# One fixed-order region over the whole kernel, and six order strings laid out anew

## Chip, core and metric

The kernel runs on one core of a Trainium2 chip. The core has five engines that run side by side, each with its own instruction stream and waits on semaphores: TensorE (PE, matmuls; PEld is its weight load), VectorE (DVE), ScalarE (ACT), GpSimd (POOL) and SyncE (SP, which issues most of the DMAs). The metric is the device time of one launch in microseconds. The kernel before takes 396.76 us, the median of 3 runs (395.31 to 397.34).

## The reference

Four residual layers over x of shape 1 x 2048 x 512: attention, convolution, and both again with the same weights.

```python
def _A_ref(x, wqkv, wo):            # 32 heads of 16
    qkv = (x @ wqkv) ...
    off = jnp.arange(8) * 2         # 8 keys per row: itself and every second row behind it
    logits = jnp.einsum("bhsd,bhswd->bhsw", q, kg) * scale
    attn = _softmax(jnp.where(mask, logits, -1e9), axis=-1)
    o = jnp.einsum("bhsw,bhswd->bhsd", attn, vg)
    return o.reshape(B, S, D) @ wo

def _B_ref(u, A_re, A_im, B_re, B_im, C_re, C_im, log_dt, Dskip):
    P = jnp.exp(logdA[:, :, None] * l[None, None, :])
    K = jnp.einsum("dn,dnl,dn->dl", Cc, P, dB).real      # the kernel of a state space model
    Yf = rfft2(pad(u)) * rfft2(pad(K))
    return irfft2(Yf)[..., :L] + u * Dskip

x = x + _A_ref(_layernorm(x), A_wqkv, A_wo)
x = x + _B_ref(_layernorm(x), ...)
x = x + _A_ref(_layernorm(x), A_wqkv, A_wo)
x = x + _B_ref(_layernorm(x), ...)
```

## The kernel before

The program runs through six parts, one after the other, with the seams overlapped. The order of each part is a string in which a letter, or a letter with digits, stands for one step.

- k_gen (0 to about 104 us, string ORDERK) makes the convolution kernel K from tables of powers, and at the same time normalises x, transposes it and projects keys and queries. Its last steps are the first products of query and shifted key for the attention that follows.
- LayerA.core (about 104 to 180 us, string CORE0) is the first attention. For each of four query blocks q and four feature tiles ft, `mult` (letter m) multiplies the queries with 8 shifted copies of the keys on DVE (line 342, tile prod, two buffers); `lsum` (l) sums the products over a head's 16 features on PE with 8 matmuls (line 350) or 32 (line 354) into the logits L; `mx` (x) takes the maximum (line 414); then follow the exponential, the sum, the reciprocal and the normalised weights attn. `q_proj` (q) and `v_proj` (v) each do one projection of four matmuls (lines 223 and 398), which ACT casts out (lines 225 and 400). When the last rows of v are there, two DMAs copy v_ext shifted by one partition (lines 403 and 404). `pv_mult` (P) multiplies weights and shifted values on DVE (line 472, tile pav), `pv_sum` (S) sums on PE (lines 487 and 497), `out_proj` (O) projects (line 508).
- FftB.run with ORDER0 (about 180 to 237 us) is the first convolution, through transforms as matmuls: f1 (line 811; its outputs a1s are cast at line 800), f2 (line 818), `u_f2` (U, cast ub at line 869), the product with the spectrum of K `u_mult` (u, line 857, on DVE), and back with i1 (m, lines 883 and 887) and i2 (y and v, lines 931 to 933, then the sum into x_sb at lines 935 and 937). The spectrum of K (kf) is made here once and stored to kf_dram.
- ORDERF (about 237 to 262 us) ends the first convolution together with the layer norm, transposes (T; lines 271 and 273) and key projections (P; lines 282, 285 and 295) of the second attention. A digit behind a letter is a block or a tile.
- LayerA.core with CORE1 (about 262 to 343 us) is the second attention; `load_w2` issues 32 loads of w_sb on SP (line 596).
- FftB.run with ORDER1 (about 343 us to the end) is the second convolution. It loads the stored spectrum: `kf_load` issues three DMAs for each of 16 pieces (lines 847 and 849), up to 10 pieces ahead of the products, into the tiles named kf_ring, w_sb and kx. `store` writes finished rows to the output.

What sets the order of the work: `tc.manual_schedule(engines=...)` keeps the engines that it names in the order in which the program issues to them. Outside such a region, and across its edges, the scheduler may move instructions. MAN names DVE, ACT, PE and SP; MAN_ALL adds POOL. Before, there is one region with MAN_ALL around k_gen, and four with MAN: around the first core, around ORDER0, around ORDERF and CORE1 together, and around ORDER1. The loads of one DMA queue are issued in the queue's order: an issue that waits holds up those behind it.

## Time and profile before

The profiled execution has a span of 393.9 us; the median of the runs is 396.76 us, so some 2.9 us lie around the span.

| what | value |
|---|---|
| median of 3 runs | 396.76 us |
| span of the profiled execution | 393.9 us |
| DVE's instructions | 449 |
| share of DVE in the span | 95% |
| DMA moved | 54.18 MB, 138 GB/s on average |

The chain of work that ended last, which is followed back from the last instruction to what released each step, stands on these engines:

```profile
PE 49%; DVE 21%; ACT 19%; issue 5%; DMA 2%; SPq 2%; POOL 1%; DVEq 0%; ACTq 0%; POOLq 0%
```

The costliest lines on DVE are these; after the bar come the busy time and the mean of one in nanoseconds, then the idle time ahead of them and what ended it:

```profile
L472 DVE TENSOR_TENSOR pav<-attn,v_ext 128x4096 bf16<-128x4096 bf16 (+1 forms) x34 | 72.3, 2160 | 0.3 <-DMA v_ext<-v_ext 0.3
L342 DVE TENSOR_TENSOR prod<-qT,kT_ext 128x4096 bf16<-128x4096 bf16 x29 | 65.6, 2288 | 3.0 <-PE L L350 2.1
L1119 DVE TENSOR_TENSOR A_t<-A_t,pow_t 128x1024 bf16<-128x1024 bf16 (+4 forms) x46 | 38.2, 873 | 0.2
```

### The profile page before, as it was taken

The page shows a single profiled execution, that of the slowest core. Times are in us where ns is not written, and L with a number is a line of the kernel's source. Part 1 is how long each engine was busy: PE and PEld are TensorE (multiplying, and loading weights), DVE is VectorE, ACT ScalarE, POOL GpSimd, SP SyncE. Part 2 cuts the span into 40 slices and gives each one's busy share as a digit, 9 for nine tenths or more (in the row PEclk, how much of TensorE's full clock was granted, in tenths as well). Part 3 has the DMA queues.
Part 4 walks back from the last instruction along what each step waited for, and adds up shares of the span by engine and source line. Part 5 has one row for each costly group of instructions (what it writes and reads, how often), then busy time and mean ns, then how long its engine had stood idle before and what let it go on. Part 6 is the DMA issues. An engine that isn't in the chain of part 4 may idle for free.

```text
span 393.9 us, 14769 instructions
## 1 busy us (share of the span) xinstructions
PE 324.1 (82%) x6451; PEld 231.5 (59%) x6499; DVE 372.8 (95%) x449; ACT 331.1 (84%) x568; POOL 65.5 (17%) x97
## 2 busy tenths in 40 slices
PE   3000258999999999999998899999999999998894
PEld 2000116756734676766887888543456676677894
DVE  6999999999989999999999989979999999989984
ACT  7999999997558799899999998574666779889992
POOL 9402960000280000010731201100000020000000
PEclk9999999999999999999999999999999999999999
DMA  7953810414027556277678634820253057604525
GB/s 209 396 155 50 83 53 3 106 28 108 9 66 198 128 168 176 61 228 235 215 265 300 216 110 110 300 62 2 73 141 96 3 170 222 195 13 155 171 68 152
DMA packets 68303, 54.18 MB, mean 138 GB/s; under 512 B 33545, under 2 KB 58670, under 8 KB 67982
## 3 DMA queue, kind: packets, MB, share of 16 engines
q1 hardware_dynamic: 66566, 48.70, 42.7%
q0 software_dynamic: 1664, 4.52, 3.1%
q8 instruction: 51, 0.84, 0.9%
q14 instruction: 14, 0.11, 0.1%
q10 hardware_dynamic: 8, 0.00, 0.0%
HBM read 30.15 MB, written 13.24 MB: 110 GB/s over the span
## 4 chain that ended last, share of the span: by engine, by line
PE 49%; DVE 21%; ACT 19%; issue 5%; DMA 2%; SPq 2%; POOL 1%; DVEq 0%; ACTq 0%; POOLq 0%
PE pq L398 7%; PE po L497 5%; PE pq L508 4%; PE pq L223 4%; PE pk L1277 3%; DVE A_t L1119 3%; ACT ub L869 3%; DVE B_t L1119 3%; PE L L354 3%; PE pp L282 3%; ACT a1s L800 3%; PE pp L1215 2%; DVE t L857 2%; SPq L596 2%; PE L L350 2%
## 5 line engine op out<-in xcount | busy, mean ns | idle before, releaser
L472 DVE TENSOR_TENSOR pav<-attn,v_ext 128x4096 bf16<-128x4096 bf16 (+1 forms) x34 | 72.3, 2160 | 0.3 <-DMA v_ext<-v_ext 0.3
L342 DVE TENSOR_TENSOR prod<-qT,kT_ext 128x4096 bf16<-128x4096 bf16 x29 | 65.6, 2288 | 3.0 <-PE L L350 2.1
L1119 DVE TENSOR_TENSOR A_t<-A_t,pow_t 128x1024 bf16<-128x1024 bf16 (+4 forms) x46 | 38.2, 873 | 0.2
L1205 PE MATMUL pt<-ident,x_blk 128*128 128x128 bf16 x64 | 6.0, 241 | 39.4 <-ACT x_blk L195 39.4
L508 PE MATMUL pq<-wop,oT 128*128 128x512 bf16 x121 | 31.5, 379 | 2.4 <-issue 1.9
L497 PEld LDWEIGHTS <-pav 64*128 64x128 bf16 x1728 | 26.9, 95 | 9.9 <-DVE pav L472 3.3
L869 ACT CAST ub<-pb 128x1024 bf16<-128x1024 f32 x32 | 32.6, 1110 | 0.0
L1215 PE MATMUL pp<-xnT,kT_ext 128*128 128x512 bf16 x88 | 25.5, 413 | 7.3 <-ACT xnT L1208 4.3
L818 PE MATMUL pb<-a1s,w_sb 128*128 128x64 bf16 x768 | 27.4, 193 | 3.8 <-ACT ub L869 1.4
L398 PE MATMUL pq<-wv,xnT 128*128 128x512 bf16 x123 | 30.0, 379 | 0.5 <-ACT kgs L1285 0.3
L497 PE MATMUL po<-ident,pav 64*128 64x64 bf16 x1728 | 29.9, 190 | 0.6 <-ACT oT L499 0.2
L400 ACT CAST v_ext<-pq 128x512 bf16<-128x512 f32 x32 | 18.7, 586 | 13.5 <-PE pq L398 11.1
L800 ACT CAST a1s<-pb 128x1024 bf16<-128x1024 f32 x29 | 28.5, 1063 | 1.2 <-PE pb L811 1.2
L1205 PEld LDWEIGHTS <-x_blk 128*128 128x128 bf16 x64 | 4.6, 107 | 41.3 <-ACT x_blk L195 40.2
L818 PEld LDWEIGHTS <-w_sb 128*128 128x128 bf16 x768 | 25.1, 98 | 6.0 <-issue 4.0
L178 POOL TENSOR_TENSOR ln_rstd<-ln_rstd,ln_mh 128x4 f32<-128x4 f32 x2 | 4.0, 1995 | 120.1 <-DVE ln_rstd L177 66.9
L1277 PEld LDWEIGHTS <-A_t 128*64 128x64 bf16 (+1 forms) x512 | 21.7, 103 | 3.8 <-DVE A_t L1119 0.2
L800 DVE CAST a1s<-pb 128x1024 bf16<-128x1024 f32 x19 | 22.5, 1220 | 1.4 <-PE pb L811 1.0
L1277 PE MATMUL pk<-B_t,A_t 128*64 128x84 bf16 (+1 forms) x512 | 23.5, 201 | 0.2
L223 PE MATMUL pq<-xnT,kT_ext 128*128 128x512 bf16 x85 | 22.6, 379 | 0.9 <-issue 0.5
L225 ACT CAST qT<-pq 128x512 bf16<-128x512 f32 x24 | 14.0, 585 | 9.8 <-PE pq L223 9.5
L398 PEld LDWEIGHTS <-xnT 128*128 128x128 bf16 x128 | 11.9, 97 | 15.3 <-issue 2.4
(264 smaller groups left out, 919.9 us busy)
## 6 DMA issues: line engine op xcount, KB each, us to landing
w_sb<-w_dram SPq DMA_DIRECT2D x64, 128.0 KB, 3.0
w_dram<-xnT SPq DMA_DIRECT2D x1, 4096.0 KB
kf_ring<-kf_dram SPq DMA_DIRECT2D x13, 256.0 KB, 3.8
kf_ring<-kf_dram SPq DMA_DIRECT2D x26, 128.0 KB, 3.6
v_ext<-v_ext SPq DMA_DIRECT2D x4, 784.0 KB, 6.1
x_blk<-in_A_x_dram SPq DMA_DIRECT2D x4, 512.0 KB, 4.7
kT_ext<-in_A_wqkv_dram SPq DMA_DIRECT2D x4, 512.0 KB, 9.2
x_sb<-in_A_x_dram SPq DMA_DIRECT2D x4, 512.0 KB, 6.3
```

Of the source, the lines that this page charges most:

```text
L223: nc.tensor.matmul(pq[:], lhsT=self.wqk[:, dt, ft * P:(ft + 1) * P], rhs=self.xnT[:, dt, q * 512:(q + 1) * 512], start=(dt == 0), stop=(dt ...
L342: nc.vector.tensor_tensor(pr, self.qT[q][:, ft].unsqueeze(1).to_broadcast([P, W, 4, P]), kap, ALU.mult)
L398: nc.tensor.matmul(pp[:], lhsT=xnT[:, dt, a * P:(a + 1) * P], rhs=wv[:, dt, :], start=(dt == 0), stop=(dt == NDT - 1))
L472: nc.vector.tensor_tensor(pv[:, i], attn[:, n % 4].unsqueeze(2).to_broadcast([P, W, DH // parts, H]), vap, ALU.mult)
L497: nc.tensor.matmul(po[:, h, 0, i * nt + ft, :], lhsT=pvf[rows, i, w, ft * P:(ft + 1) * P], rhs=ident[rows, rows], start=(w == 0 and ft + i ...
L508: nc.tensor.matmul(pw[:], lhsT=oT[:, ftp, :], rhs=self.wo[:, ftp, :], start=False, stop=(ftp == NDT - 1))
L800: (self.nc.scalar.copy if eng == "act" else self.nc.vector.tensor_copy)(dst, src)
L818: nc.tensor.matmul(p2[:, j, :], lhsT=self.w2[:, ec * EC + j, :], rhs=a1s[:, ec * EC + j, :], start=True, stop=True)
L869: nc.scalar.copy(ub[:], p2)
L1119: return lambda: nc.vector.tensor_tensor(*args)
L1215: nc.tensor.matmul(pps[kind, b, ft][:], lhsT=la.wqk[:, dt, c:c + P], rhs=la.xnT[:, dt, b * 512:(b + 1) * 512], start=(dt == 0), stop=(dt = ...
L1277: nc.tensor.matmul(o, lhsT=lhs, rhs=Bt[:, ri, c * CH + ql].rearrange("p b g -> p (b g)"), start=(not half and j % 4 == 0 and ri == 0), sto ...
```

## The change

It has two halves. One `manual_schedule` with MAN is opened at the start of the function and stays open to its end; around k_gen a second one adds POOL alone, and the later regions become `if True:`. And all of the six order strings have their steps in another order; each string holds the same steps as often as before, so each engine runs the same instructions. LATE0, ROWS and ENGK stay. Lines behind the strings are one lower in the kernel after.

```diff
 ORDER0 = """
-KD KA KA KA KA KD KD KA KA KD kA KD KA KD KA kA kD UA KD UA UD UA UA UD UA UD
-kA KD kA kD u kD u m u kA kD UA UA m u kD UA kD m UA UA u m kD UA m
...
+KD KA KA KA KA KD KD KA KA KD KD kA kA kD KA KD KA KD UA UA UD UA KD UA UD UA UD kA kA kD u kD kA u
+m kD u m m UA u u kD u kD UA m m UA UA u m UA kD UA u UD UA m m kA kA u kD kA yD u u YA m YA m u m
...
 ORDER1 = """
-UD UA UA UD UA UD UA UD UA UD UA u UD m u m u u m UA u UA m u UD m
-UA m u m u u m u m u u m YA YD u YA m m yA YD m u u YA u YA
-YA m m m w001A w000D yA yA w011D YA w010D yA yD yA yD yA v102D v101A v112D v111A v113D v103D v100A v110D
+UD UA UA UD UA UD UA UD UA UD UA u UD u m u UA UA m UD m u u u m u m m UA m u m u u m u u m YA YD u
+YA m m yA YD u u m w001A u YA YA m YA m m w000D yA YA YA w010D yA yD yA yD yA v102D w011D v100A
+v110D v112D v113D v103D v101A v111A
 """
 CORE0 = """
-vmvvvvqlvmxvlmemvvrclvnlmqTlqmxmvvelvvvvcmlqcPlSPrqOmncml1VTxPPqeSmr2lqP4OlSOSm5PqOP3S7lmOSnlPOx
-VPeOPSPrOSnPO6SObbP9SwOP8SPdBHOVaOPfSEdObatSaCaAfataGDFO
+mmvvvvlvmvqlxmlevvmqvrllcnqqTmvvxlvvmvvvPqePclmSmlmrcO6lxncVqPTPeSOOPqSrl3SmP5qml4OS2OPlmS7nlPOx
+PVeOSbrOPSnPOSbP18OSPPOdSBOV9aEPdOPSfObGaCaFatfASOtaHaDw
 """
 CORE1 = """
-0m1l2ml3mqvvmvllqvmqvxqelmlvmmvvqrlnqlmTvmxPPvlvvqvvqvmlmvqlqelmSrqnxmPSPqTOSOSlePOlPmrSOSnmOOPl
-bSlPSPwOxdfPVaePOSraPOnVabPOSPdOSOPSbPOSfaOftSdafaaftO
+0mv21lm3lqvvmvmqllmvqqvmvxllvqevqmmrlmlvnvvmxTvqPlvlPvmveqqrmlSmnlSqxTPqOPmlSeqOSOOmPlrSPnbPlSOP
+SmOOSlPOxwVeOdrPSfPbnPVOadPaSOSPafOPSbOPaSfdaOSfataftO
 """
...
     nc = tc.nc
+    ctx.enter_context(tc.manual_schedule(engines=MAN))
...
-    with tc.manual_schedule(engines=MAN_ALL):
+    with tc.manual_schedule(engines={ET.Pool}):
         C = k_gen(tc, nc, ...
...
-    with tc.tile_pool(name="ctmp_g2", bufs=1) as g2tmp, tc.manual_schedule(engines=MAN):
+    with tc.tile_pool(name="ctmp_g2", bufs=1) as g2tmp:
...
-    with tc.manual_schedule(engines=MAN):
+    if True:
         late["."] = lambda: None
         fb.run(ORDER0, u, k=kp, late=[late[c] for c in LATE0.split()])
```

ORDERK (four lines of 96 letters) and ORDERF (the end of the first convolution) are permuted in the same way, and the regions around ORDERF with CORE1, and around ORDER1, become `if True:` too.

More of the change, by code (lines that the diff above doesn't have):

```diff
@@ L46 @@
 ORDERK = """
-sbiCCiCisCGiCbiMsaibsCbMiibMcMsTibMGicGMMbasMGiGibTMTMbsGGTabbiTTiaTsicGTbbacTiTibcGsTMTGiaGaMlM
-TbasMlWaiaMlyMMwyyiMiayMsttbeMkTaaaMadeMaiMkkaMKMTalMbMkMlWMMqMKqlqMqMMMyyQMHQyqqUQkkpyakKaUkKqt
-pUtUxUexqpQUaekdkUqUUaxaqUKUpUUk3axHUl3EkplTKpTWQ3Tl3xlTxTyppWyqyqkHxTlytkTTQqUzzeKqUTteQUkTkTKE
-kUTzkzUkTxkTKttkKkUkUkpKekekxKUUpkkKqxpKUqUUxUkUoEUUkpQkUKkpxUUoxpUXpxXKopxxZXZZ
+siCbCiCsibiCisibbMCsiMaiCMMbsTcaiMibbMTGTisMibbGsTcGbiMibaGMTiTsMcbcaTibaTTbiTasMMGaacaMiMGbaGla
+MaGGMMlGMGTwWMaTsiaTlyyMTayTylitMtaelqeWMMkMksMliqMQbykMMykKiMdKqyMqyaMQktMMtdMqkbMMHqeapKpxUUUU
+aUxapQapUqqkUkU3HaU3eUUQTxKUkkTqaUlqKxTkUkpQTTaxl3TEppW3TlqxpyKTyqykHTlytkTUUTWUtQTKeUUlqqkTUQkT
+UekKkkUUKxkKkzkkkzxzzppKtxeUUtpUkeKUkkkxxpKUkUKooUExpqUqkUpKUokkxEUpKXxQXpxxZXZZ
 """
 ORDER0 = """
-KD KA KA KA KA KD KD KA KA KD kA KD KA KD KA kA kD UA KD UA UD UA UA UD UA UD
-kA KD kA kD u kD u m u kA kD UA UA m u kD UA kD m UA UA u m kD UA m
-u u UD UA m u kA u m m kA kD kA m yD u m u YA m u YA yD u u m
-m YA u m u m w000A m YA yA YD YA yA yD yA w010D yA
+KD KA KA KA KA KD KD KA KA KD KD kA kA kD KA KD KA KD UA UA UD UA KD UA UD UA UD kA kA kD u kD kA u
+m kD u m m UA u u kD u kD UA m m UA UA u m UA kD UA u UD UA m m kA kA u kD kA yD u u YA m YA m u m
+yD u u m u m w000A m m u YA YA yA m YD YA yA yD yA w010D yA
 """
@@ L59 @@
 ORDERF = """
-yD h00 h01 yA YA v101A v100A v110A v111A h10 z12A a0 p0 v113A h11 a1 p1 z02A S z03A n0D T0 n1G E00D
-v103D E01A P03 H2 a2 T1 P01 E10D p2 E11D Q00 n2G H3 P00 a3 P02 P11 P12 p3 T2 E21D E20D P10 P13
-P22 P20 n3D T3 E31A P23 P21 E30D x1
+yD yA YA h01 v101A h00 v100A v110A h10 a0 v111A v113A p0 z02A S h11 z03A a1 p1 z12A n0D T0 n1G E00D
+v103D H2 E01A P00 T1 Q00 P03 a2 E10D p2 P02 E11D P13 n2G H3 a3 P01 P11 T2 E20D p3 P12 E21D P10 P20
+n3D P23 T3 E31A E30D P22 x1 P21
 """
 ORDER1 = """
-UD UA UA UD UA UD UA UD UA UD UA u UD m u m u u m UA u UA m u UD m
-UA m u m u u m u m u u m YA YD u YA m m yA YD m u u YA u YA
-YA m m m w001A w000D yA yA w011D YA w010D yA yD yA yD yA v102D v101A v112D v111A v113D v103D v100A v110D
+UD UA UA UD UA UD UA UD UA UD UA u UD u m u UA UA m UD m u u u m u m m UA m u m u u m u u m YA YD u
+YA m m yA YD u u m w001A u YA YA m YA m m w000D yA yA YA w010D yA yD yA yD yA v102D w011D v100A
+v110D v112D v113D v103D v101A v111A
 """
 CORE0 = """
-vmvvvvqlvmxvlmemvvrclvnlmqTlqmxmvvelvvvvcmlqcPlSPrqOmncml1VTxPPqeSmr2lqP4OlSOSm5PqOP3S7lmOSnlPOx
-VPeOPSPrOSnPO6SObbP9SwOP8SPdBHOVaOPfSEdObatSaCaAfataGDFO
+mmvvvvlvmvqlxmlevvmqvrllcnqqTmvvxlvvmvvvPqePclmSmlmrcO6lxncVqPTPeSOOPqSrl3SmP5qml4OS2OPlmS7nlPOx
+PVeOSbrOPSnPOSbP18OSPPOdSBOV9aEPdOPSfObGaCaFatfASOtaHaDw
 """
 CORE1 = """
-0m1l2ml3mqvvmvllqvmqvxqelmlvmmvvqrlnqlmTvmxPPvlvvqvvqvmlmvqlqelmSrqnxmPSPqTOSOSlePOlPmrSOSnmOOPl
-bSlPSPwOxdfPVaePOSraPOnVabPOSPdOSOPSbPOSfaOftSdafaaftO
+0mv21lm3lqvvmvmqllmvqqvmvxllvqevqmmrlmlvnvvmxTvqPlvlPvmveqqrmlSmnlSqxTPqOPmlSeqOSOOmPlrSPnbPlSOP
+SmOOSlPOxwVeOdrPSfPbnPVOadPaSOSPafOPSbOPaSfdaOSfataftO
 """
@@ L1494 @@
     la.front_w()
-    with tc.manual_schedule(engines=MAN):
+    if True:
         la.front_open()
@@ L1548 @@
     fb.open_mid()
-    with tc.manual_schedule(engines=MAN):
+    if True:
         out_v = out.rearrange("b (p a) d -> p (b a) d", p=P)
```

## The prediction

> **What bounds the kernel now.** I read the page's busy times first, then the busy time of each engine in stretches that match the kernel's parts, then VectorE's waits, and last the timelines around the places where the order changes.

> ```profile
> PE 324.1 (82%) x6451; PEld 231.5 (59%) x6499; DVE 372.8 (95%) x449; ACT 331.1 (84%) x568; POOL 65.5 (17%) x97
> PEclk9999999999999999999999999999999999999999
> ```

> VectorE (DVE) works 372.8 of 393.9 us. The change keeps every instruction, so DVE's 372.8 us stay and the most that any order could save is its 21.1 us of idle time. The stretches say where that idle lies; the columns are the length, then PE, PEld, DVE, ACT and POOL busy, the granted clock, DMA share and GB/s:

> ```profile
> 0.00:104.00 104.00, 53.35 (x651) 36.29 (x660) 99.74 (x167) 94.25 (x175) 31.89 (x46) 1.00 0.44 113
> 104.00:112.00 8.00, 7.68 (x85) 3.81 (x84) 6.42 (x5) 4.14 (x8) 5.95 (x11) 1.00 0.21 55
> 112.00:180.00 68.00, 65.65 (x1359) 42.37 (x1375) 67.67 (x44) 58.87 (x117) 6.17 (x11) 1.00 0.54 152
> 180.00:240.00 60.00, 55.26 (x1596) 50.00 (x1597) 58.12 (x75) 59.49 (x73) 15.03 (x25) 1.00 0.64 219
> 240.00:262.00 22.00, 21.37 (x175) 13.64 (x176) 19.21 (x59) 15.04 (x30) 3.50 (x4) 1.00 0.59 187
> 262.00:300.00 38.00, 37.48 (x376) 18.53 (x382) 36.76 (x21) 22.51 (x37) 0.00 (x0) 1.00 0.27 73
> 300.00:343.00 43.00, 41.73 (x1171) 29.79 (x1175) 42.39 (x35) 35.15 (x83) 2.94 (x1) 1.00 0.44 134
> 343.00:378.00 35.00, 31.19 (x749) 27.07 (x744) 33.60 (x43) 33.71 (x43) 0.00 (x0) 1.00 0.34 106
> 378.00:394.00 16.00, 10.37 (x334) 9.96 (x324) 8.91 (x10) 7.96 (x10) 0.00 (x0) 0.98 0.46 134
> ```

> The reader is to see that the bound moves. Up to 104 and in the two attention cores (112 to 180, 300 to 343) DVE is full; in 180 to 240 ACT is (59.49 of 60); in 240 to 300 PE is (21.37 of 22, 37.48 of 38); the last 16 us are a chain. Of DVE's idle 4.3 us lie before 104, 7.1 after 378, and 9.8 between, in pieces. DVE's largest waits in the middle name their causes:

> ```profile
> DVE x_sb L935 <- PE pb L933: 2.5, 6, 0.8
> DVE prod L342 <- PE L L350: 2.1, 2, 1.6
> DVE kT_ext L295 <- ACT kT_ext L285: 1.3, 2, 1.2
> DVE xnT L273 <- PE pt L271: 1.2, 2, 1.1
> ```

> **The change part by part.** *The region.* DVE's, ACT's and POOL's orders come from the strings in both kernels; compiled with the old strings, the single region moves only two things.

> First, the handoff from k_gen to the first core:

> ```profile
> 108.25 0.61 PE L350 MATMUL L<-A_pr,ind 128*32 128x512 bf16 x8
> 108.79 0.39 PE L398 MATMUL pq<-wv,xnT 128*128 128x512 bf16 x1
> 109.11 0.62 PE L350 MATMUL L<-A_pr,ind 128*32 128x512 bf16 x8
> 109.78 2.29 DVE L342 TENSOR_TENSOR prod<-qT,kT_ext 128x4096 bf16<-128x4096 bf16 x1 [1.57 <-PE L L350]
> ```

> Eight v_proj matmuls (L398) that the scheduler had put between the three groups of logit sums (L350) now come after the third. The groups then wait only for their products; the last of these ends at 108.0, a group lasts 0.6, so the product at 109.78 can start at about 108.83: DVE gains 0.95 us. PE pays: it stands from about 107.0 to 108.1, 1.1 us, where it did projections before. DVE is full behind this place, so a gain there carries on until some PE result is late: the next gates are the first pav (its shifted v_ext lands when DVE has about 0.3 left) and the last maximum of the logits at 138.8, which waits for PE. Bounds 0 and -0.95; I take -0.5, the middle, because half of the gates on the way hang on the engine that is later.

> [...]

> Second, SyncE's (SP's) queue in layer 1. Before, the load of g_sb and 7 of the first 10 kf_ring triples went out at 245.75 to 289, the two v_ext shifts between them. Now these 22 issues stand behind the shifts and the 32 w_sb loads. Rows:

> ```profile
> 281.46 0.67 SPq L403 DMA_DIRECT2D v_ext<-v_ext  x1
> 316.60 18.38 SPq L596 DMA_DIRECT2D w_sb<-w_dram  x32
> 337.19 0.52 SPq L847 DMA_DIRECT2D w_sb<-kf_dram  x1
> 337.75 1.30 SPq L849 DMA_DIRECT2D w_sb<-kf_dram  x2
> 357.06 0.45 SPq L847 DMA_DIRECT2D kf_ring<-kf_dram  x1
> ```

> A triple takes about 1.9 us to issue (337.2 to 343.5 for three is 2.1, 246.13 to 255.2 for four 2.3 at most, 357.06 to 358.9 is 1.85); from 335.4 on the ten are issued by 335.4 + 10 x 2.0 = 355.4, and kf_ring's next loads, which wait for the product at 357, are not passed over. Landing takes 2.5 to 5.9 us from issue. Load n is there at 337.4 + 2.0n + 5.9 at worst, and needed at 355.8 + 1.15n (L857's products): for n = 9, 361.3 against 367.2 (two casts in between). So 0, covered by 6 us; without that cover it is a rival below. The bounds are 0 and +3.8.

> *ORDERK.* DVE is full to 104; what moves is within its queue. The one gate that tightens is the table copy by ACT at 61.8: its slack of 0.6 us becomes -0.8 if ACT's work is merely counted up, but ACT had that much idle before it. Zero, bounds -0.3 and +0.5.

> *CORE0, ORDER0, ORDERF.* In the two latter the waits of 1.05 at 258 (PE, L271) and 1.16 at 260.8 (ACT, L285) have the same producers with the same work ahead of them; moves elsewhere stay within one or two instructions and cross no gate with less than 0.3 us. Zero, bounds -0.5 and +0.5.

> *CORE1.* Here PE is the bound and has no gaps, so a place in its order is a time. Projections of four matmuls (0.87 us each by PE's rows) were moved ahead of groups of L350. DVE's products wait for these, since their buffers come free only then:

> ```profile
> 271.76 2.29 DVE L342 TENSOR_TENSOR prod<-qT,kT_ext 128x4096 bf16<-128x4096 bf16 x1 [0.27 <-ACT v_ext L400]
> 282.78 4.49 DVE L342 TENSOR_TENSOR prod<-qT,kT_ext 128x4096 bf16<-128x4096 bf16 x2 [0.49 <-PE L L350]
> 303.23 4.49 DVE L472 TENSOR_TENSOR pav<-attn,v_ext 128x4096 bf16<-128x4096 bf16 x2 [0.26 <-DMA v_ext<-v_ext]
> ```

> Counting the work ahead of each, the L350 group that releases the product at 267.0 moves 0.9 later (it had 0.3 to spare: DVE +0.6), the one for 271.76 by 1.7 (0.1 to spare), for 277.79 by 1.3 (0.1), for 282.78 by 1.7 (0.1). These overlap, they don't add: DVE is 0.5, 1.2, 0.9 and 1.4 late there, and about 1.0 at the maximum at 299.55. At 303 a pav goes ahead of a product and the wait of 0.26 goes. From 303 to 343 DVE has 0.6 us of idle, so it can't catch up. I take +1.1; bounds 0 (if PE's queue has slack that the records miss) and +1.6, the largest single delay.

> *ORDER1.* To 378 DVE's order is the same but for one cast. In the tail a group of 16 matmuls (L931 to L933, 0.9 us) and its DVE sum go from ahead of the last inverse transforms (L887) to behind them. The chain of waits there is PE alone, so what DVE waited for at 379.7 (0.81) and 381.5 (0.56) comes 0.9 earlier; but the moved 0.9 us of PE are still owed before the last sum at 388.41. What can be won is what PE stands idle before that sum: its records after 378 add up to 10.37 us, all of 378 to 388.4, but counted at the pace of gapless matmuls (0.06 us for those of 128 columns) the work after 378.9 is 9.2 us, which ends at 388.1. I take -0.4, the 0.3 and a little for the shorter last sums; bounds -0.8 and +0.3.

> The sum: -0.5 + 0 + 0 + 0 + 1.1 - 0.4 = +0.2. The profiled span of 393.9 becomes 394.1; the median before is 396.76, 2.9 above the span, so 397.0 us.

> **The rivals.** A difference under 0.5%, 2 us, can hardly be told from none here, so the forecast is "same".

> *The gains carry, CORE1 is not later.* For it: the new order has several operands landing just as DVE comes for them (the pav ahead of the product at 303 starts as the second v_ext shift lands), as if PE had time to give there. Against it: four gates with 0.1 to 0.3 us of slack. -0.95 at the handoff, -0.5 in ORDER0 and ORDERF, -0.8 in the tail, 0 in CORE1, -0.3 in ORDERK: -2.55, so 394.2 us.

> *The late loads.* The single region puts the kf_ring loads behind w_sb. If a triple costs over 2.6 us with w_sb's own traffic still moving, load 9 comes later than its product (337.4 + 9 x 2.6 + 5.9 = 366.7 against 367.2): that is the point from which it decides. At 3.07 us (512 KB at the 170 GB/s of the slice with w_sb) it is 370.9, DVE 3.8 us late, and ACT and PE behind it: 400.5 us. Against it: the triples at 337 to 343 took 1.9 to 2.1 right behind the same w_sb loads.

> [...]

> *CORE1's delays add.* Each product waits for a sum and each sum for a product; if PE also stands at the late products, the 1.6 is paid twice, +3.2, with -0.9 at the handoff and in the tail not won since DVE comes late to both ends: 400.0 us. For it: PE has only 0.5 us of idle in 262 to 300. Against it: there are two product buffers, so a product is two groups ahead.

> *The region does nothing.* Then the handoff's gain and the queue's risk go; 397.5 us, and not told from the forecast.

> **How the numbers follow.** Forecast with the region rival 0.40, gains carry 0.30, late loads 0.13, delays add 0.17. Faster needs 394.8 or less: 0.30. Slower needs 398.7 or more: 0.30. The forecast's own range is 395.4 to 398.6. All terms at their lower bounds give 394.2, and the runs of before reach 1.45 us below their median; all but the queue's at their upper bounds give 396.8 + 0 + 0.5 + 0.5 + 1.6 + 0.3 = 399.7, and the late loads 400.5. I give 393.2 to 400.8.

> **What would show it.** Handoff: the L342 product that waited 1.57 us waits about 0.6. CORE1: waits of L342 on L350 between 265 and 285 that sum to over 1.5 us, and the last L472 some 1 us nearer the end of the span than the start would let it be. Queue: no wait of L857 on kf_ring. Tail: the waits of L935 on L933 fall from 2.5 to under 1.8. I am wrong if L857 waits for a DMA, if ACT's stretch 180 to 240 grows by over 0.5 us, or if CORE1's waits vanish.

## The result, and the profile after

The changed kernel is slower: 406.94 us, the median of 4 runs (404.60 to 408.59), against 396.03 us for the kernel before, run beside it (4 runs). The ratio is 1.0275, with a 95% interval from 1.0241 to 1.0308, so about +10.9 us. The forecast was 397.0 us, no change, with a range to 400.8. The profiled execution of the kernel after has a span of 405.6 us.

The line of busy times and the clock line of the page after, to be held against those of before:

```profile
PE 327.2 (81%) x6456; PEld 235.0 (58%) x6499; DVE 373.2 (92%) x449; ACT 331.0 (82%) x568; POOL 58.9 (15%) x97
PEclk9999998999999999999999999999998999999898
```

DVE's work is the same, 373.2 against 372.8 us; what was added is idle time, 32 us in place of 21. And the clock line, which was all 9s, has four places with 8 in it: the granted clock is halved from 61.09 to 64.50 us, from 306.85 to 310.26, from 375.12 to 378.53, and from 402.42 to the end. Six of the nine stretches of before, shifted with the work (the columns are the length, then PE, PEld, DVE, ACT and POOL busy, the granted clock, DMA share and GB/s):

```profile
0.00:107.00 107.00, 53.20 (x627) 35.70 (x634) 99.21 (x167) 93.22 (x173) 25.23 (x46) 0.98 0.43 110
107.00:115.00 8.00, 7.59 (x103) 4.54 (x102) 7.59 (x5) 4.29 (x8) 4.76 (x9) 1.00 0.14 37
266.00:306.00 40.00, 38.44 (x422) 19.85 (x427) 37.49 (x22) 23.49 (x39) 0.00 (x0) 1.00 0.18 47
306.00:351.00 45.00, 41.85 (x1073) 29.39 (x1085) 41.96 (x35) 34.01 (x81) 1.03 (x1) 0.96 0.38 116
351.00:388.00 37.00, 31.89 (x761) 28.11 (x755) 33.60 (x43) 33.38 (x42) 0.00 (x0) 0.95 0.76 235
388.00:406.00 18.00, 11.26 (x358) 10.71 (x355) 9.30 (x11) 8.69 (x11) 0.00 (x0) 0.90 0.40 119
```

The same work takes 3 us more up to the handoff, 1 us more in the first core (not shown) and 2 us more in each of the last four stretches; only the handoff (107 to 115) is better, with 0.4 us of DVE's idle time in place of 1.6. Two things to see in the last three lines: the granted clock of 0.96, 0.95 and 0.90, and the DMA share of 0.76 in the second convolution, where it was 0.34. The 0.90 costs nothing: PE's last matmul is over at 399.3, ahead of the last halved period.

Both kernels run the same DVE work, so the time at which DVE has done a given amount of it tells how late the new kernel is at each place of the program. Worked out from the two traces, in us after minus before:

```
place in the kernel before     DVE late by
k_gen, at 20 us                -0.1
k_gen, in the middle           +1.9
k_gen, end                     +2.8
handoff done                   +1.6
core 0, at 130                 +2.5
core 0, end                    +2.7
ORDER0, end                    +3.5
ORDERF, end                    +3.9
CORE1, at 296                  +5.3
CORE1, at 325                  +7.8
CORE1, end                     +7.9
ORDER1                         +9.6
tail                           +10.8
```

DVE's waits name the first losses (the columns are us in all, how often, and the longest):

```profile
DVE prod L341 <- PE L L349: 2.9, 4, 1.0
DVE a1s L799 <- PE pb L810: 2.3, 3, 1.0
DVE A_t L1118 <- DMA pow_t<-pow_t: 2.1, 1, 2.1
...
DVE B_t L1118 <- ACT B_t L1106: 1.1, 1, 1.1
```

The wait of 2.1 us for pow_t is new, and it is a wait for a DMA's landing in k_gen. The same product in the kernel before, and in the kernel after:

```profile
25.66 0.28 DVE L1119 TENSOR_TENSOR A_t<-A_t,pow_t 128x256 bf16<-128x256 bf16 x1
```

```profile
24.92 0.49 DVE L1118 TENSOR_TENSOR A_t<-A_t,pow_t 128x256 bf16<-128x256 bf16 x2 [2.06 <-DMA pow_t<-pow_t]
```

The largest new wait on PE has no producer at all; the view of PE's waits and the timeline of PE show it:

```profile
PE po L496 <- issue: 2.8, 2, 2.5
```

```profile
307.28 1.54 PE L496 MATMUL po<-ident,pav 64*128 64x64 bf16 x51 [2.52 <-issue]
```

PE stops at 304.76 after 13 matmuls of a group of 64 and goes on with the other 51 at 307.28, though all that they read has long been there. In steps of 1 us (columns as above: PE, PEld, DVE, ACT, POOL busy, clock, DMA share, GB/s):

```profile
300.00:301.00 1.00, 1.00 (x14) 0.68 (x14) 1.00 (x2) 0.83 (x2) 0.00 (x0) 1.00 0.65 169
301.00:302.00 1.00, 1.00 (x48) 0.98 (x47) 1.00 (x1) 0.39 (x2) 0.00 (x0) 1.00 1.00 250
302.00:303.00 1.00, 1.00 (x63) 0.89 (x56) 1.00 (x2) 0.06 (x1) 0.00 (x0) 1.00 1.02 271
303.00:304.00 1.00, 1.00 (x32) 0.83 (x31) 1.00 (x1) 0.99 (x2) 0.00 (x0) 1.00 0.75 200
```

```profile
305.00:306.00 1.00, 0.00 (x0) 0.00 (x0) 1.00 (x2) 0.00 (x0) 0.00 (x0) 1.00 0.00 0
306.00:307.00 1.00, 0.00 (x0) 0.00 (x0) 1.00 (x2) 0.00 (x0) 0.00 (x0) 0.93 0.00 0
307.00:308.00 1.00, 0.72 (x29) 0.71 (x29) 1.00 (x1) 0.00 (x0) 0.00 (x0) 0.50 0.00 0
309.00:310.00 1.00, 0.84 (x2) 0.30 (x2) 1.00 (x1) 0.45 (x1) 0.00 (x0) 0.50 0.00 0
```

From 301 to 303 PE starts 48 and 63 matmuls in a microsecond, and in just that time the second v_ext shift fills the DMA engines (share 1.00). Then PE stands, with no wait that the profile shows, and the clock is halved from 306.85 to 310.26. The records of the DMA queues point to code as what ran out. PE has some 13,000 instructions, and the page of either kernel lists a DMA queue of kind "instruction" with 51 packets, 0.84 MB: one packet of 16 KB for every 255 instructions. Counting PE's instructions in program order, the packets start around the time at which PE passes instruction 194 of each 256, most of them within 2 us (46 of 51 in the kernel before, 39 in the kernel after); call that the time at which the packet is due. From 65 us on the kernel before has no stall of PE of over 0.35 us without a producer, the kernel after has three, and each begins at instruction 194 of the next 256; the first is 0.87 us at 194.9, and these are the others:

```
kernel  packet   due     starts  ends    PE at the next 194   PE stands
before  33       296.9   297.3   298.8   302.4                -
after   33       301.3   304.8   305.9   304.8                2.52, to 307.28
after   43       356.9   359.8   360.7   361.1                1.17, to 362.22
```

In the kernel before, packet 33 goes out just ahead of the v_ext shift (at 297.3; the shift's first data packet starts at 297.5). In the kernel after it comes due in the middle of the shift and waits until the shift is through; PE meanwhile uses up its 256 instructions in 3.4 us. It doesn't go out when the mean DMA share falls, which is 0.16 from 304 to 305, but at 304.77, where the shift's very last data packet ends.

From 65 us on no packet of the kernel before makes PE stand for over 0.35 us, and 3 packets of the kernel after do; the worst of these 3 costs 2.52 us of PE's time.

### The profile page after: what moved, and what is told of

Its sections match the earlier page's. It is cut to its first block, busy times and chain, and to the rows that moved or that the text cites. A ratio compares the mean times of both kernels' runs of the same rounds, so it can differ in the third digit from the quotient of the medians.

```text
span 405.6 us, 14776 instructions
## 1 busy us (share of the span) xinstructions
PE 327.2 (81%) x6456; PEld 235.0 (58%) x6499; DVE 373.2 (92%) x449; ACT 331.0 (82%) x568; POOL 58.9 (15%) x97
## 4 chain that ended last, share of the span: by engine, by line
PE 48%; DVE 8%; issue 5%; SPq 4%; ACT 4%; DMA 2%; DVEq 0%; ACTq 0%
PE pq L397 7%; PE pq L222 5%; PE po L496 5%; PE pq L507 4%; SPq L595 4%; PE pp L281 3%; DVE t L856 3%; PE L L353 3%; PE pb L817 3%; PE pb L882 3%; PE pb L810 2%; DMA kf_ring<-kf_dram 2%; ACT a1s L799 2%; PE pb L886 2%; PE L L349 2%
## 5 line engine op out<-in xcount | busy, mean ns | idle before, releaser
L496 PE MATMUL po<-ident,pav 64*128 64x64 bf16 x1728 | 30.9, 192 | 2.9 <-issue 2.8
L222 PE MATMUL pq<-xnT,kT_ext 128*128 128x512 bf16 x90 | 23.6, 386 | 0.7 <-issue 0.5
L498 ACT CAST oT<-po 128x512 bf16<-128x512 f32 x27 | 15.5, 576 | 8.2 <-PE po L496 8.2
```

Source lines behind the costliest of these rows:

```text
L222: nc.tensor.matmul(pq[:], lhsT=self.wqk[:, dt, ft * P:(ft + 1) * P], rhs=self.xnT[:, dt, q * 512:(q + 1) * 512], start=(dt == 0), stop=(dt ...
L496: nc.tensor.matmul(po[:, h, 0, i * nt + ft, :], lhsT=pvf[rows, i, w, ft * P:(ft + 1) * P], rhs=ident[rows, rows], start=(w == 0 and ft + i ...
```

## The experiments

Each was run in 3 rounds beside the kernel before. "Late" is DVE's lateness as in the table above.

**The two halves of the change apart.** e1 has before's six strings and after's region; e2 after's strings and before's regions.

```diff
e1: the kernel after
-siCbCiCsibiCisibbMCsiMaiCMMbsTcaiMibbMTGTisMibbGsTcGbiMibaGMTiTsMcbcaTibaTTbiTasMMGaacaMiMGbaGla
+sbiCCiCisCGiCbiMsaibsCbMiibMcMsTibMGicGMMbasMGiGibTMTMbsGGTabbiTTiaTsicGTbbacTiTibcGsTMTGiaGaMlM
...
e2: the kernel after
-    ctx.enter_context(tc.manual_schedule(engines=MAN))
...
-    with tc.manual_schedule(engines={ET.Pool}):
+    with tc.manual_schedule(engines=MAN_ALL):
...
-    if True:
+    with tc.manual_schedule(engines=MAN):
```

> The kernel before with the single region alone, all six strings as before. Theory (the loss sits in the strings: late k_gen tables, a code refill of TensorE that comes late in CORE1, and what follows): the handoff gains about 1 us, the kf_ring loads now run right behind w_sb and may make one refill late (0 to 1.2 us), so 395 to 397 us against 396. Rival (the region is the cause, through the kf_ring loads that share the DMA engines with the second convolution): 400 us or more.

398.25 us, ratio 1.0066 (1.0032 to 1.0101): between the two expectations. The profiled execution is the longest of the seven, 399.85 us. In it the handoff gains 1.0 us and has given back 1.7 by 130; PE then stands 1.38 us at 342.5 and 0.87 at 356.0, both at instruction 194 or 195 of 256, as the kf_ring loads run.

> The new strings in the four regions of before. Theory: nearly all of the loss stays, less the refill stall of 1.2 us at 361 that goes with the early kf_ring loads, plus the handoff's 1 us that is not won: 404 to 407 us, with the TensorE stall of 2.5 us in mid group near 305 still there. Rival (the region is the cause): 396 to 399 us.

406.26 us, ratio 1.0296 (1.0244 to 1.0348). The strings alone cost what the whole change costs. The profiled execution is the shortest of the five, 402.26 us: the stall in mid group is there (1.57 us at 304.4) and the clock isn't halved behind it; the stall at 361 is gone, as expected.

**One string put back.** e3 is the kernel after with before's CORE1, e4 with before's ORDERK.

```diff
-0mv21lm3lqvvmvmqllmvqqvmvxllvqevqmmrlmlvnvvmxTvqPlvlPvmveqqrmlSmnlSqxTPqOPmlSeqOSOOmPlrSPnbPlSOP
-SmOOSlPOxwVeOdrPSfPbnPVOadPaSOSPafOPSbOPaSfdaOSfataftO
+0m1l2ml3mqvvmvllqvmqvxqelmlvmmvvqrlnqlmTvmxPPvlvvqvvqvmlmvqlqelmSrqnxmPSPqTOSOSlePOlPmrSOSnmOOPl
+bSlPSPwOxdfPVaePOSraPOnVabPOSPdOSOSPbSPOSfaOftSdafaaftO
```

> The kernel after with CORE1 as before. Theory: what DVE loses from 262 to 323 (1.4 before the refill stall, 2.6 behind it) goes, w_sb's loads start 13 us less late against the old order; 401 to 403 us, and no TensorE stall above 0.5 us without a producer near 305. Rival (lateness is made up or made elsewhere whatever CORE1 does): 405 us or more.

402.48 us, ratio 1.0162 (1.0102 to 1.0222), as expected. From 196 to 340 there is no stall without a producer, and DVE is 3.5 us late at 262 and still 3.5 at 343. Behind that there are three such stalls, of 1.18, 1.17 and 0.52 us, between 344 and 364.

> The kernel after with ORDERK as before. Theory: the wait of 2.1 us of A_t for pow_t's copy and the 1 us for B_t go, and DVE is full behind them so the gain reaches the end: 403 to 404.5 us. Rival (later PE-bound stretches take the lateness up): 406 us or more.

407.69 us, ratio 1.0300 (1.0230 to 1.0369). The theory missed: DVE is 2.5 us less late at the end of k_gen, and the median doesn't move. Its profiled execution, the shortest of its four at 403.85 us, shows a wait that the kernel after does not have: DVE's product L856 waits 2.4 us for a kf_ring load. e13 takes this up.

**The region's two places apart.** e5 joins only the regions around k_gen and the first core, e6 only those around ORDERF with CORE1 and around ORDER1.

```diff
+    seam = ExitStack()
+    seam.enter_context(tc.manual_schedule(engines=MAN))
-    with tc.manual_schedule(engines=MAN_ALL):
+    with tc.manual_schedule(engines={ET.Pool}):
         C = k_gen(tc, nc, ...
...
+    seam.close()
```

> The kernel before with its regions around k_gen and the first core joined, so that the three L350 groups of the handoff stand together; the seam in layer 1 stays as before. Theory (the gain of 1 us at the handoff is given back by 130, since TensorE is the engine that comes late there): between 0 and +1 us against before, so 395.3 to 396.3. Rival (the handoff is a net gain that another part of the region change hides): 394.5 or less.

396.31 us, ratio 1.0023 (0.9999 to 1.0047). DVE's timeline in e5 shows how the gain goes:

```profile
108.80 4.50 DVE L342 TENSOR_TENSOR prod<-qT,kT_ext 128x4096 bf16<-128x4096 bf16 x2 [0.51 <-PE L L350]
114.77 1.23 DVE L414 TENSOR_REDUCE mx<-L 128x128 bf16<-128x1024 f32 x1 [1.48 <-PE L L325]
```

The product starts at 108.80 in place of 109.78 and waits 0.51 us in place of 1.57. But the maximum behind it, which started at 114.19 with no wait, now waits 1.48 us for PE, and starts at 114.77.

> The kernel before with only the regions around ORDERF with CORE1 and around ORDER1 joined: all engines but SP in the order of before, the g_sb and kf_ring loads behind w_sb. Theory (traffic of these loads makes TensorE's code refill late while f1 and f2 use up 256 instructions in some 3 us): one or two TensorE stalls at instruction 194 of 256 between 340 and 360, 0.8 to 1.4 us each, +1 to +2.5 us: 396.3 to 398. Rival (the loads themselves come late): waits of L857 on a DMA. Second rival (free): 395.3 +- 0.5, no such stalls.

397.18 us, ratio 1.0046 (1.0014 to 1.0078), in the range expected. Its profiled execution was the longest of its ten, 402.28 us; there PE stands 2.33 us at 343.5, at instruction 194, and no L857 waits for a DMA. This execution lies 5.1 us above the median, and 2.1 us of it are a wait in k_gen for the load of x_blk, so it doesn't show what the median execution pays for late code.

**The suspected cost alone.** e7 is the kernel before, every engine in its order, with DMAs that nobody waits for, right behind the loads of w_sb.

```diff
+    aside = dram.tile([2, NG, NEC, 64, 2, DQG, EC], BF16, name="aside_dram")
...
+            for n in range(10):
+                for h in range(2):
+                    nc.sync.dma_start(aside[h, n // NEC, n % NEC], kf_dram[n // NEC, n % NEC])
```

> The kernel before, every engine in its order, with 20 more DMAs of 256 KB from kf_dram to an unused DRAM tile on SP's queue right behind the w_sb loads (335 to 347 us): work added that nobody waits for. Theory (refill of code suffers from other transfers): stalls of TensorE at instruction 194 of 256 between 338 and 356 with no producer, +0.5 to +2.5 us. Rival (the stalls come from the density of the instructions alone): no stall, within 0.5 us of before.

398.54 us, ratio 1.0084 (1.0052 to 1.0116): more than expected. PE stands 1.42 us at 352.8, at instruction 195, with no producer:

```profile
PE pb L811 <- issue: 1.4, 1, 1.4
```

The packet of code was due at 348.5 and started at 351.9. In the kernel before it was due at 348.1 and started at 349.0, and PE had no stall. No L857 of e7 waits for a load. So in e7 transfers that nothing depends on came with a late packet of code and 1.42 us of standing PE. The profiled execution is the shortest of the six, 396.33 us; what the others lose beyond this stall isn't seen.

**The other side: fewer instructions in the same time.** e8 is the kernel after with two projections, of 4 long matmuls each, moved into the run of short ones at 301 to 305.

```diff
-...veqqrmlSmnlSqxTPq...
+...veqrmlqSmnqlSxTPq...
```

> The kernel after with two projections of CORE1 (8 matmuls, 1.7 us of TensorE time) moved into the run of small matmuls at 301 to 305. Theory (256 short instructions are used up in 3.4 us, before the refill that waits for the v_ext shift lands): the stall of 2.52 us falls to 0.5 to 1.2, the clock isn't halved at 307, and the kernel takes 402 to 405 us. Rival (a stall of another kind, or one that is made up later): 406 to 408 us.

402.76 us, ratio 1.0190 (1.0142 to 1.0237), as expected: 0.85%, or 3.4 us, less than the 1.0275 of the kernel after, by two moves in one string. The two intervals don't overlap, if barely. PE's timeline and the windows of e8:

```profile
305.79 0.97 PE L496 MATMUL po<-ident,pav 64*128 64x64 bf16 x55 [0.73 <-issue]
```

```profile
306.00:307.00 1.00, 1.00 (x59) 0.95 (x51) 1.00 (x2) 0.20 (x1) 0.00 (x0) 1.00 0.06 16
307.00:308.00 1.00, 0.95 (x9) 0.55 (x8) 1.00 (x1) 1.00 (x2) 0.00 (x0) 1.00 0.00 0
```

The stall is 0.73 us and the clock stays at 1.00. DVE's lateness goes from 3.7 at 296 to 4.4 at 325, in place of 5.3 to 7.8.

**One string new in the kernel before.** e9 takes CORE1, e10 ORDER1 and e11 ORDERK from the kernel after; e12 is the other way round, the kernel after with these three as before.

```diff
e9: the kernel before
-0m1l2ml3mqvvmvllqvmqvxqelmlvmmvvqrlnqlmTvmxPPvlvvqvvqvmlmvqlqelmSrqnxmPSPqTOSOSlePOlPmrSOSnmOOPl
+0mv21lm3lqvvmvmqllmvqqvmvxllvqevqmmrlmlvnvvmxTvqPlvlPvmveqqrmlSmnlSqxTPqOPmlSeqOSOOmPlrSPnbPlSOP
...
e10: the kernel before
-YA m m m w001A w000D yA yA w011D YA w010D yA yD yA yD yA v102D v101A v112D v111A v113D v103D v100A v110D
+v110D v112D v113D v103D v101A v111A
...
```

> The kernel before with the new CORE1 alone, four regions. Theory (L350 groups moved behind projections make DVE 1.0 to 1.5 us late from 265 to 300; the run of small matmuls then empties TensorE's instruction store near 300 while the v_ext shift is under way, with or without the clock gate): +2.5 to +5.5 us, 398 to 401. Rival (CORE1 costs only in company with the other strings): 396 to 397.

399.61 us, ratio 1.0107 (1.0042 to 1.0172), as expected. PE stands in the same way, and the clock is halved at 303:

```profile
304.56 1.56 PE L497 MATMUL po<-ident,pav 64*128 64x64 bf16 x51 [2.49 <-issue]
```

```profile
303.00:304.00 1.00, 0.00 (x0) 0.00 (x0) 1.00 (x2) 0.00 (x0) 0.00 (x0) 0.62 0.00 0
304.00:305.00 1.00, 0.44 (x18) 0.45 (x20) 1.00 (x1) 0.00 (x0) 0.00 (x0) 0.50 0.00 0
```

In that execution, the longest of the four, DVE's lateness goes from +3.6 at 296 to +7.4 at 325, and the clock is halved for two periods, from 303.24 to 310.07. Some 1.8 us of the 3.6 are not CORE1's. They arise in k_gen, whose string is that of before:

```profile
73.73 0.69 DVE L138 BATCH_NORM_STATS2 ln_bn<-x_blk 128x6 f32<-128x512 bf16 x1 [1.86 <-DMA x_blk<-in_A_x_dram]
```

The load is issued at 69.57 in place of 67.92, behind a stretch (60.90 to 64.31) in which the clock is halved. Of the runs with before's ORDERK only e9 and e6 have a halved clock there, and only they have a wait of over 0.5 us for x_blk. The shortest run of e9 has a mean clock of 1.000 and takes 396.46 us; the other three have 0.985 to 0.994 and take 399.24 to 402.13. So the 1.07% is a mean over runs with a lower granted clock and one without.

> The kernel before with the new ORDER1 alone. Theory (ORDER1's loss in the changed kernel comes from late code refills and the halved clock, not from its order): within 0.7 us of before, 394.7 to 396.1, as the prediction's term of -0.4 has it. Rival (its order itself makes TensorE wait for ACT's cast of a1s near 365, some 2 us): 397 to 399.

396.82 us, ratio 1.0036 (1.0014 to 1.0058): neither expectation. Two of its waits, of PE and of DVE:

```profile
PE pb L818 <- ACT a1s L800: 3.3, 6, 2.1
```

```profile
DVE x_sb L935 <- PE pb L933: 2.1, 3, 1.7
```

Before, PE waited 1.2 us for ACT's a1s, 0.3 at the longest. The new order makes PE stand 2.1 us once; in the tail one wait of 1.7 stands where there were six of up to 0.8.

> The kernel before with the new ORDERK alone. Theory (A_t's first products are put ahead of the landing of pow_t's copy, 2.0 us, and B_t's ahead of its cast, 1.0 us, in a stretch where DVE is full): +2 to +3 us, 397.4 to 398.4. Rival (later stretches that another engine bounds take it up): 395.3 to 396.3.

397.78 us, ratio 1.0075 (1.0048 to 1.0102), as expected:

```profile
DVE A_t L1119 <- DMA pow_t<-pow_t: 2.3, 1, 2.3
```

> The kernel after with ORDERK, CORE1 and ORDER1 as before; what stays new is the region, CORE0, ORDER0 and ORDERF. Theory (the region costs 2.6 us as measured alone, the other three strings at most 1.2): 397.5 to 399.5. Rival (the losses lie in the strings that stay new): 402 or more.

397.63 us, ratio 1.0059 (1.0033 to 1.0085), as expected.

**What was still open.** e13 is e8 with before's ORDERK, e14 the kernel before with the new CORE0, ORDER0 and ORDERF; strings alone are exchanged, as in the diffs above.

> The kernel after with the thinned CORE1 of the run before and ORDERK as before. Theory (ORDERK's 2.4 us, measured alone, add to the other parts; the earlier run with ORDERK put back lost them again only through TensorE stalls and halved clocks that the thinned CORE1 avoids): 399.5 to 401.5 us against 402.8 with the thinned CORE1 alone. Rival (with the other new strings the k_gen time is taken up later whatever CORE1 does): 402.3 to 403.5.

405.34 us, ratio 1.0238 (1.0194 to 1.0282): both expectations missed, the kernel is no faster than e8, whose interval overlaps this one. ORDERK's gain is gone early: DVE is 1.2 us less late than in e8 at the end of k_gen, and no less late at 262. Then comes a new loss. A wait of DVE, and lines of SP's and DVE's timelines in e13:

```profile
DVE t L856 <- DMA kf_ring<-kf_dram: 2.6, 2, 2.4
```

```profile
324.50 17.63 SPq L595 DMA_DIRECT2D w_sb<-w_dram  x32
...
378.17 0.54 SPq L846 DMA_DIRECT2D kf_ring<-kf_dram  x1
378.76 1.23 SPq L848 DMA_DIRECT2D kf_ring<-kf_dram  x2
```

```profile
382.82 2.54 DVE L856 TENSOR_TENSOR t<-ub,kf_ring 128x2048 bf16<-128x2048 bf16 x2 [2.40 <-DMA kf_ring<-kf_dram]
```

SP's queue has become a bound of its own. It starts w_sb when the last products of query and key in CORE1 are through (324.50 here, 329.84 in the kernel after, 316.60 before), needs 17.6 us for w_sb, and then has all 16 triples of the spectrum before it, to 380; before, 7 of them were long done. The last products get their loads at 382.8 at the earliest, however early DVE comes. In the kernel after the queue ends at 384.0 and the last four products start at 383.85, with no wait: the queue was just covered by the other losses, and who takes some of these away uncovers it. e8 has it too, with 1.7 us in three waits. PE then waits 3.2 us for the late product, and the clock is halved at 386.

> The kernel before, four regions, with the new CORE0, ORDER0 and ORDERF alone. Theory (these three strings are neutral: the run that kept them and the region new lost 0.59 per cent where the region alone lost 0.66): within 0.8 us of before, 394.6 to 396.2. Rival (they cost 1.2 us as DVE's lateness in the changed kernel grows from 2.7 at 184 to 3.9 at 264): 396.3 to 397.2.

397.48 us, ratio 1.0034 (1.0004 to 1.0063): the rival is nearer, these three strings cost some 1.3 us.

None of the versions beats the kernel before.

## Why the prediction was wrong

Measured alone, the parts cost 0.66% (the region), 0.75% (ORDERK), 1.07% (CORE1), 0.36% (ORDER1) and 0.34% (CORE0, ORDER0, ORDERF): 3.2%, or 12.6 us, against 2.75% for all together. The intervals of the single parts are 0.9 to 2.6 us to either side, and the parts don't simply add, as e4 and e13 show. Step by step:

- *ORDERK, taken at 0.* It costs 0.0075 x 395.4 = 3.0 us. The prediction counted the engines' work ahead of each operation and looked at one gate, ACT's table copy, which indeed costs nothing; it did not set DVE's new order against the landing of pow_t's copy. A_t's product moved ahead of the time when that copy is there, and DVE, which is full, waits 2.1 to 2.3 us. Another 1.1 us go to a gate that it didn't look at: ACT's cast of B_t comes late, behind a cast that waits 1.46 us for PE.
- *The handoff, -0.5.* DVE's gain of 1.0 us is there and PE pays as was said. But the first gate behind it is a maximum 5 us later, not the first pav or the maximum at 138.8; it waits 1.48 us for PE. Net 0 to +1.9 us in e5 (0.9 in the middle).
- *SP's queue, 0, covered by 6 us.* The reckoning of the first ten loads holds: no product of the kernel after waits for a load. (One cast lies between the first and the tenth product, not two; the 367.2 us are what the trace has.) The step failed twice over. It looked at the loads' own landing alone, and with their traffic PE stood at instruction 194 or 195 of 256: 1.42 us in e7, with other traffic alone; 1.38 and 0.87 us in e1 and 2.33 us in e6, in executions that were their longest. And w_sb's start was taken as before's 316.6, where the new CORE1 puts it at 329.84: the queue stands 13 us later there, and 8 us later in e13, where it has become a bound. The rival of late loads named the right place, but its price was not what the changed kernel paid.
- *CORE1, +1.1.* The delays from the L350 groups are there, +1.4 from 264 to 296, inside the bounds; they overlap, as was said, and the rival that they add to 3.2 is not what the trace shows. What the prediction lacked is what follows at 301: a run of short matmuls that is through 256 instructions in 3.4 us, a packet of code that starts 3.5 us late, a stall of 2.52 us and a clock halved for 3.41 us, another +2.5. The step that failed is "DVE can't catch up, so +1.1 is carried": it took PE's pace as given by its work. CORE1 alone costs 4.2 us (e9: 0.0107 x 395.4), give or take 2.6.
- *ORDER1, -0.4.* It costs 1.4 us alone. The PE work owed in the tail was counted; the wait of 2.1 us for ACT's cast near the start of the part was not, since only the tail was walked through.
- *CORE0, ORDER0, ORDERF, 0.* +1.3 us alone, outside the bounds of 0.5.
- *The clock.* The prediction's table has the clock at 1.00 in every stretch to 378. That holds from 58.9 us on; ahead of that there is no record, and matmuls go at half the pace (last section). It did not look for places where PE would stand long; the new order has two of over 2 us after 300 (2.52 us for code, 2.12 us for ACT's cast from 371.7 on), and the clock is halved at 307 and at 375.

The signs that the prediction named for being wrong did not come: no product waits for a load, ACT's busy time from 184 to 244 is 58.2 us where it was 59.5, and DVE's waits in CORE1 are there. They watched the steps that it had walked through, and the loss came from those it had not. Of the signs for being right, the tail's is missed: the waits of the last sums for PE are 2.0 us, not under 1.8. The 2.9 us that were put around the span compare two executions (within the profiled one of the kernel after they are 1.7); the forecast doesn't hang on them.

The larger error is one of method: from a tight order, whose gates have 0.0 to 0.3 us of slack, nearly every move costs, and a sum of best guesses near zero overlooks what a walk leaves out: landings of DMAs, the code, the clock.

What stays open: the time from the end of a packet of code to PE's first matmul (1.4 to 1.5 us in the three stalls of the kernel after) has no cause that these runs show. That the halved clock makes most of the difference between the runs of one kernel is only argued: the kernel after has a mean granted clock of 0.997 in its shortest run, 404.60 us, and 0.982 to 0.984 in the other three, and e2 and e9 are alike in this. No run changes the clock and nothing else. Most of the loss of the kernel after can't be the clock's, since its shortest run, whose mean is short by less than one halved period, is still 8.6 us above the median of before.

## What to carry to other kernels

When an order is laid out for a kernel with thousands of short matmuls, check two things that no engine's own work shows: whether a packet of TensorE's code comes due while a large transfer is under way (in the kernel after one did at 301.3, in the v_ext shift, and PE stood 2.52 us), and whether anything makes TensorE stand (stands of 1.81, 2.52 and 2.12 us came with a halved clock in the kernel after, one of 2.1 us in e2 did not). Here two groups of long matmuls, moved in among the short ones, were worth more than operands that came a little earlier (3.4 us in e8). And a loss that is taken away can uncover a queue that was just hidden behind it, so parts measured alone need not add.

## What the runs showed of the hardware

TensorE's code shows in the traces as packets of a DMA queue of kind "instruction": 51 packets of 16 KB, one for every 255 instructions of PE, which last 0.9 to 2.0 us in the kernels before and after. In the kernel after one of them started 3.5 us late behind the v_ext shift, where the shift's last data packet ends (304.77), and in e7 one started 3.4 us late beside copies of DRAM to DRAM. At the three stalls of the kernel after, PE resumed 1.4 to 1.5 us after the packet's end.

The mean granted clock of a run can mislead. The profiled run of e10 has a mean of 0.937 and took 396.54 us, about its median. Its records name 10.54 to 58.32 as halved; those of the kernel before begin only at 58.88, and its mean is 0.999. But in the kernel before, too, matmuls of 128x128 follow each other every 107 ns ahead of 58 us (13 of them from 47.21) and every 56 ns behind it (8 from 65.36). It ran those at half the pace, and its mean doesn't show it.
